# Crossbar transposes of z, split score exponentials and earlier PV steps in a fused attention and MLP kernel

## The chip, the core and the metric

The kernel runs on one core of a Trainium2 chip. The metric is the device time in microseconds (us) of one execution. Before the change it was 321.34 us, the median of three runs (319.71 to 322.16). Names used below: PE is TensorE, ACT is ScalarE, DVE is VectorE, POOL is GpSimd; SP is the engine whose queue issues most of the DMA transfers. The clock given with a profile is the share of TensorE's full clock that was granted; "half clock" means that this share was 0.5.

## The reference

```python
# q, k, v: (8 batches, 8 heads, 576 tokens, 64), fp32
scores = q @ k.T / 8, kept where 0 <= pos_q - pos_k < 64, else -1e9   # window of 64
attn   = softmax(scores) @ v                                          # per head
x      = attn, heads side by side: (8, 576, 512)
xn     = (x - mean) / sqrt(var + 1e-6) * g_ln
out    = x + relu(xn @ w_ch1) @ w_ch2                                 # 512 -> 2048 -> 512
```

## The kernel before

The kernel works in batches of 512 tokens. While TensorE runs the MLP of batch g, the attention of batch b = g + 1 runs beside it, in gaps that the program text fixes. (The last 64 tokens of all batches, the "tails", form a ninth MLP batch.) An MLP batch in the steady part is a row of 30 units: 16 first-layer units ("hps": four matmuls of 512 columns and one Relu on ScalarE), then 14 product units of eight 256-column matmuls (wX, wY, wZ). After each unit the program may place attention work in a slot. In the names of the tiles, sc are scores and pt their exponentials; PV is the product of pt with v, its result is xps; vA is v in fp16 and vB its copy shifted by 64 rows; xn is the attention's output, mv its mean and variance and rs the factor made from the variance; z is the normalized row block and zT its transpose, which the MLP reads. The "presums" are VectorE's sums and differences (sw1 to sw4) of parts of the first layer's result hrT, which the products need; osb is the output tile. The two hps buffers are what ties PE to ScalarE: a unit can start only when the Relu of the unit two before has emptied its buffer.

```python
def l1(hc):                                   # one hps unit
    hps = ps_mm.tile([128, 512], FP32, ...)   # pool of 2 buffers
    for kc in KCS: nc.tensor.matmul(out=hps, lhsT=w1g[...], rhs=zT[g][:, kc, :], ...)    # L409
    nc.scalar.activation(out=hrT[:, hc, :], in_=hps, func=AF.Relu, ...)                  # L413
# ... (cut)
def b_step(g, kb):                            # PV of one score step, then the norm's statistics
    # 16 matmuls xps <- pt, vA or vB (L313); VectorE: rcp, xn, stats, mv
def r_step(g, kb):                            # two tiny ScalarE instructions, wait for mv
    nc.scalar.activation(out=rs, in_=mvs[(g, kb)][:, 1:2], func=AF.Ln, ...)              # L332
    nc.scalar.activation(out=rs, in_=rs, func=AF.Exp, ...)                               # L333
def z_step(g, kb): ...                        # VectorE: z <- xn, mv, rs   (128 x 512, fp16)
def zt_step(g, kb):                           # 4 PE transposes and one ScalarE copy
    for kc in range(NKC): nc.tensor.transpose(out=ztp[:, kc, :], in_=z[...], ...)        # L357
    nc.scalar.copy(out=zT[g][:, :, 128 * kb:128 * kb + 128], in_=ztp)                    # L360
def make_vB(b):                               # shift of v by 64 rows, from GpSimd's queue
    nc.gpsimd.dma_start(out=vB[b][64:128, :], in_=vA[b][0:64, :])
    nc.gpsimd.dma_start(out=vB[b][0:64, 1:4], in_=vA[b][64:128, 0:3])
# ... the schedule of one steady batch (cut): slot numbers are units
for j in range(4):
    at((0, 6, 11, 17)[j], s_mm, b, j)         # scores and both exponentials
    at((1, 7, 12, 18)[j], s_mask, b, j)
    bz((6, 11, 17, 23)[j], b, j)              # b_step, then r_step and z_step one and two units on
    at((12, 17, 23, 28)[j], zt_step, b, j)
at(1, load_qk, n, 0); at(2, load_qk, n, 1); at(5, load_v, n, 0, 4)   # SP's queue, n = b + 1
at(11, x_main, n, 0); at(13, x_main, n, 1)                            # SP: crossbar transposes of q, k
at(26, make_vB, n)
```

In the traces here SP issues its transfers in the order of the program (below, the loads of 178.87 go out behind the transposes that stand before them), so a transfer that waits for its data holds up whatever the program has put behind it.

The softmax here doesn't subtract the row's maximum and nothing guards it: scores larger than these inputs give would overflow.

## Time and profile before

| | before |
|---|---|
| time, median of 3 runs | 321.34 us |
| span of the profiled run, clock | 319.0 us, 0.998 |
| steady batch, from its first hps matmul to the next one's | 30.95 us, four times |
| of it PE's short waits for a Relu | 0.645 us |
| of it the bare queue of PE | 30.31 us |

The third row is read from the start times of the first hps matmul of each batch. The fourth takes more care, because the modelled matmul ends hide short waits: for each unit I take the distance from its start to the next one's and subtract what the same kind of unit needs when nothing holds it. "Waits" below always means this excess. PE's own list of waits in this profile shows none of those 0.645 us.

### The profile page before, as it was taken

The numbers are of one execution on the slowest core, as the hardware profiler recorded it, in microseconds if no ns is written. First come the engines' busy times: TensorE is split into PE (matmuls) and PEld (weight loads), VectorE is DVE, ScalarE is ACT, GpSimd is POOL, SyncE is SP. The second block draws the span as 40 slices with busy tenths as digits, with TensorE's granted clock in tenths as the row PEclk, the third lists the DMA queues.
The fourth block names the chain that finished last, engine by engine and source line by source line (L and its number), as shares of the span: only waits on it lengthen the run. The fifth ranks groups of instructions, "written<-read, shape, count | busy, mean of one in ns | idle before, by whom it ended". The sixth has DMA issues, their size and how long they took to land.

```text
span 319.0 us, 7507 instructions
## 1 busy us (share of the span) xinstructions
PE 296.9 (93%) x3047; PEld 195.5 (61%) x3047; DVE 207.4 (65%) x365; ACT 170.9 (54%) x345; POOL 128.6 (40%) x212
## 2 busy tenths in 40 slices
PE   6879998789989999999999999999999999899993
PEld 2446444378766458646864685578457854684582
DVE  0564569965996569457935893689288956771361
ACT  1699734268534763477257715851685277415600
POOL 3676667653535433452246225613444061201000
PEclk9999999999999999999999999999999999999999
DMA  7999999999997979795979688940988979203005
GB/s 177 257 369 303 333 286 288 286 285 216 142 211 159 262 117 243 145 268 135 197 153 236 149 184 211 194 101 1 251 161 143 181 188 164 51 0 134 0 2 132
DMA packets 127379, 58.35 MB, mean 183 GB/s; under 512 B 104496, under 2 KB 120368, under 8 KB 127344
## 3 DMA queue, kind: packets, MB, share of 16 engines
q1 hardware_dynamic: 123280, 46.15, 66.2%
q0 software_dynamic: 3104, 11.19, 11.4%
q10 hardware_dynamic: 960, 0.53, 0.6%
q8 instruction: 24, 0.39, 0.6%
q14 instruction: 11, 0.09, 0.1%
HBM read 38.80 MB, written 9.44 MB: 151 GB/s over the span
## 4 chain that ended last, share of the span: by engine, by line
PE 49%; DVE 12%; DMA 9%; SPq 5%; ACT 4%; issue 3%; POOL 1%; POOLq 0%
PE hps L409 19%; PE wX L483 12%; DMA tk<-in_k_dram 6%; PE wZ L483 6%; PE hph L443 3%; PE wY L483 3%; SPq L102 2%; PE xps L313 2%; DMA tv<-in_v_dram 2%; PE sc L280 2%; DVE sw L399 2%; DVE osb L498 2%; DVE stats L321 2%; DVE xn L319 2%; DVE pt L297 1%
## 5 line engine op out<-in xcount | busy, mean ns | idle before, releaser
L409 PE MATMUL hps<-zT,w1g 128*128 128x512 f16 x480 | 112.3, 379 | 1.4 <-ACT zT L360 0.3
L413 ACT ACTIVATE hrT<-hps 128x512 f16<-128x512 f32 x120 | 71.3, 596 | 31.0 <-PE hps L409 30.1
L409 PEld LDWEIGHTS <-w1g 128*128 128x128 f16 x480 | 45.0, 98 | 54.1 <-issue 6.9
L483 PEld LDWEIGHTS <-sw 128*128 128x128 f16 x512 | 49.3, 98 | 7.5 <-issue 1.1
L483 PEld LDWEIGHTS <-hrT 128*128 128x128 f16 x384 | 36.6, 98 | 6.2 <-issue 0.3
L360 ACT COPY zT<-ztp 128x512 f16<-128x512 f16 x36 | 21.0, 584 | 33.1 <-PE ztp L357 32.9
L399 DVE TENSOR_TENSOR sw<-hrT 128x1024 f16<-128x1024 f16 x32 | 22.3, 696 | 24.7 <-ACT hrT L413 24.6
L332 ACT ACTIVATE rs<-mv,epst 128x1 f32<-128x1 f32 x36 | 10.7, 296 | 44.6 <-DVE mv L323 44.6
L297 DVE TENSOR_TENSOR pt<-pt,mask 128x1024 f16<-128x1024 f16 x32 | 24.6, 772 | 14.2 <-ACT pt L284 9.2
L131 POOL CAST qk<-qk 128x1024 f16<-128x1024 f32 x22 | 23.8, 1083 | 11.9 <-DMA qk<-in_q_dram 8.6
L349 POOL CAST tok<-hrT 128x1 f32<-128x1 f16 x29 | 11.9, 410 | 37.4 <-ACT hrT L413 27.5
L443 PE MATMUL hph<-zT,w1g 128*128 128x256 f16 x192 | 23.9, 273 | 2.6 <-DVE osb L432 1.7
L321 DVE BATCH_NORM_STATS2 stats<-xn 128x6 f32<-128x512 f32 x36 | 25.0, 695 | 1.2
L319 DVE TENSOR_TENSOR xn<-xps,rcp 128x512 f32<-128x512 f32 x36 | 24.9, 692 | 1.2
L498 DVE TENSOR_TENSOR osb<-wX,xn 128x512 f32<-128x512 f32 x24 | 16.5, 688 | 13.6 <-PE wX L483 13.6
L316 DVE RECIPROCAL rcp<-xps 128x8 f32<-128x8 f32 x36 | 7.3, 203 | 25.3 <-PE xps L313 25.3
L284 ACT ACTIVATE pt<-sc 128x512 f16<-128x512 f32 x40 | 21.7, 595 | 1.7
L150 POOL CAST vA<-v 128x512 f16<-128x512 f32 x32 | 22.1, 699 | 0.8 <-DMA v<-in_v_dram 0.8
L443 PEld LDWEIGHTS <-w1g 128*128 128x128 f16 x192 | 17.9, 98 | 6.0 <-issue 2.3
L370 POOL DMA_DIRECT2D out_dram<-osb x18 | 12.6, 700 | 20.5 <-DVE osb L498 17.1
L290 ACT ACTIVATE pt<-sc 128x512 f16<-128x512 f32 x32 | 17.2, 595 | 6.0 <-PE sc L280 5.7
L343 DVE TENSOR_SCALAR z<-xn,mv,rs 128x512 f16<-128x512 f32 x32 | 19.7, 615 | 0.9 <-ACT rs L333 0.6
(76 smaller groups left out, 432.2 us busy)
## 6 DMA issues: line engine op xcount, KB each, us to landing
qk<-in_q_dram SPq DMA_DIRECT2D x16, 512.0 KB, 6.2
v<-in_v_dram SPq DMA_DIRECT2D x32, 256.0 KB, 6.2
out_dram<-osb POOLq DMA_DIRECT2D x14, 512.0 KB, 7.1
w2s<-in_moe_w_ch_dram SPq DMA_DIRECT2D x12, 512.0 KB, 6.2
qk<-in_k_dram SPq DMA_DIRECT2D x20, 256.0 KB, 5.7
qk<-in_k_dram SPq DMA_DIRECT2D x6, 512.0 KB, 6.9
w1s<-in_moe_w_ch_dram SPq DMA_DIRECT2D x4, 512.0 KB, 6.6
tk<-in_k_dram SPq DMA_DIRECT2D x8, 256.0 KB, 5.3
```

Of the source, the lines that this page charges most:

```text
L131: nc.gpsimd.tensor_copy(out=dst[:, :].rearrange("p (a j) e d -> p a e j d", j=j), in_=t[:, :].rearrange("p (a e j d) -> p a e j d", e=2, j ...
L150: nc.gpsimd.tensor_copy(out=vA[b][:, c0:c1, :, 0:D], in_=v32[b][:, c0:c1])
L284: nc.scalar.activation(out=pt[:, par].rearrange("k h w (p j) -> k (h w) p j", j=4), in_=sc[par][:, :].rearrange("k h w (j p) -> k (h w) p ...
L297: nc.vector.tensor_tensor(out=ptv, in0=ptv, in1=mb, op=ALU.mult)
L319: nc.vector.tensor_tensor(out=xn, in0=xps[:, :, 0:D], in1=rcp_b, op=ALU.mult)
L321: nc.vector.bn_stats(out=stats, in_=xn.rearrange("p h d -> p (h d)"))
L399: nc.vector.tensor_tensor(out=S[i], in0=a, in1=b, op=op)
L409: nc.tensor.matmul(out=hps, lhsT=w1g[:, kc, 128 * hc:128 * (hc + 1)], rhs=zT[g][:, kc, :], start=(kc == KCS[0]), stop=(kc == KCS[-1]),)
L413: nc.scalar.activation(out=hrT[:, hc, :], in_=hps, func=AF.Relu, bias=0.0, scale=1.0)
L443: nc.tensor.matmul(out=hps[:, e], lhsT=w1g[:, kc, 128 * hc:128 * (hc + 1)], rhs=zT[g][:, kc, 256 * half:256 * half + 256], start=(kc == KC ...
L483: nc.tensor.matmul(out=xyz[bank][:, t], lhsT=lhsT, rhs=rhs, start=bool(first and t == 0 and hc == 0), stop=(t == 1 and hc == 7), skip_grou ...
L498: nc.vector.tensor_tensor(out=o, in0=xyz[bank][:, ts], in1=x if base == "x" else o, op=ALU.add)
```

## The change

Its intent: take the sixteen groups of z transposes of the attention of batches 3 to 6 (which runs beside MLP batches 2 to 5) off PE and give them to the DMA crossbar; let a Relu in between the two exponentials of a score step; and move the PV steps forward, so that the transposed z is early enough.

```diff
-    def s_mm(g, j, pe_mask=False, pool=None):
+    def s_mm(g, j, pe_mask=False, pool=None, split=False):
 ...
+            if par == 0 or not split:
+                s_exp(g, j, par, sc[par])          # the second one comes a unit later
 ...
+    def x_step(g, kb):
+        nc.sync.dma_start_transpose(out=zT[g][:, :, 128 * kb:128 * kb + 128], in_=z)
 ...  presums of the products, slots
-                    (6, 3, 0), (10, 3, 1), (13, 1, 0), (14, 2, 0), ..., (20, 4, 0), (22, 4, 1)):
+                    (4, 3, 0), (10, 3, 1), (12, 1, 0), (12, 2, 0), ..., (22, 4, 0), (23, 4, 1)):
-                at((0, 6, 11, 17)[j], s_mm, b, j)
-                at((1, 7, 12, 18)[j], s_mask, b, j)
-                bz((6, 11, 17, 23)[j], b, j)
-                at((12, 17, 23, 28)[j], zt_step, b, j)
+                cross = g < B - 2
+                u, ub = ((0, 4, 8, 13)[j], (4, 8, 13, 18)[j]) if cross else ((0, 6, 11, 17)[j], (6, 11, 17, 23)[j])
+                if u < 15:
+                    at(u, s_mm, b, j, False, None, True)
+                    at(u + 1, s_exp, b, j)
+                    at(u + 2, s_mask, b, j)
+                else:
+                    at(u, s_mm, b, j)
+                    at(u + 1, s_mask, b, j)
+                bz(ub, b, j)
+                if cross:
+                    at(ub + 3, x_step, b, j)
+                else:
+                    at((12, 17, 23, 28)[j], zt_step, b, j)
 ...  and the tokens that pace GpSimd's casts of v: rs and the output tile in place of zT
```

More of the change, by code (lines that the diff above doesn't have):

```diff
@@ L282, in s_mm, with s_exp @@
         for par in range(2):
-            if NPE <= g < NGRP - 1:
-                nc.scalar.activation(
-                    out=pt[:, par].rearrange("k h w (p j) -> k (h w) p j", j=4),
-                    in_=sc[par][:, :].rearrange("k h w (j p) -> k (h w) p j", j=4),
-                    func=AF.Exp, bias=0.0, scale=scale,
-                )
-            else:
-                nc.scalar.activation(out=pt[:, par], in_=sc[par], func=AF.Exp, bias=0.0, scale=scale)
+            if par == 0 or not split:
+                s_exp(g, j, par, sc[par])
+        if split:
+            scs[(g, j)] = sc[1]
+    scs = {}
+    def s_exp(g, j, par=1, sc=None):
+        sc = scs.pop((g, j)) if sc is None else sc
+        pt = pts[(g, j)]
+        if NPE <= g < NGRP - 1:
+            nc.scalar.activation(
+                out=pt[:, par].rearrange("k h w (p j) -> k (h w) p j", j=4),
+                in_=sc[:, :].rearrange("k h w (j p) -> k (h w) p j", j=4),
+                func=AF.Exp, bias=0.0, scale=scale,
+            )
+        else:
+            nc.scalar.activation(out=pt[:, par], in_=sc, func=AF.Exp, bias=0.0, scale=scale)
     def s_mask(g, j):
@@ L362, in zt_step @@
             nc.vector.tensor_copy(out=dst, in_=ztp)
+    def x_step(g, kb):
+        z = zsd.pop((g, kb))
+        if g not in zT:
+            zT[g] = p_grp.tile([128, NKC, 512], FP16, tag="zT", name=f"zT_{g}")
+        nc.sync.dma_start_transpose(out=zT[g][:, :, 128 * kb:128 * kb + 128], in_=z)
     stores, cur = [], [0]
@@ L387, in t_weights @@
         nc.vector.tensor_tensor(out=o, in0=a, in1=b, op=ALU.subtract)
-    hrTs, sw = {}, {}
+    hrTs, sw, oo_of = {}, {}, {}
     def presum(g, i, c):
@@ L415, in mlp_units @@
         ch, oo = {}, {}
+        oo_of[g] = oo
         def l2(kb, part):
@@ L720 @@
             for u, i, c in ((10, 3, 0), (12, 3, 1), (14, 1, 0), (15, 2, 0), (16, 1, 1), (17, 2, 1), (20, 4, 0), (22, 4, 1)) if g == 1 else (
-                    (6, 3, 0), (10, 3, 1), (13, 1, 0), (14, 2, 0), (16, 1, 1), (17, 2, 1), (20, 4, 0), (22, 4, 1)):
+                    (4, 3, 0), (10, 3, 1), (12, 1, 0), (12, 2, 0), (16, 1, 1), (17, 2, 1), (22, 4, 0), (23, 4, 1)):
                 at(u, presum, g, i, c)
@@ L724 @@
             for j in range(4):
-                at((0, 6, 11, 17)[j], s_mm, b, j)
-                at((1, 7, 12, 18)[j], s_mask, b, j)
-                bz((6, 11, 17, 23)[j], b, j)
-                at((12, 17, 23, 28)[j], zt_step, b, j)
+                cross = g < B - 2
[10 more added lines that the diff above has]
+                    at(ub + 3, x_step, b, j)
+                else:
+                    at((12, 17, 23, 28)[j], zt_step, b, j)
         for i, f, *p in TAILS.get(g, ()):
@@ L770 @@
                 at(18, alloc_vB, n)
-                for u, c, j in ((18, 0, 1), (20, 1, 2), (24, 2, 2), (26, 3, 3)):
-                    at(u, (lambda j=j: pace(zT[b][:, 0, 128 * j:128 * j + 1])) if c % 2 == 0 else
-                       (lambda j=j: pace(rss[(b, j)])))
+                for u, c, t in ((18, 0, lambda: rss[(b, 2)]), (20, 1, lambda: oo_of[g][0][:, 0, 0:1]),
+                                (22, 2, lambda: rss[(b, 3)]), (25, 3, lambda: oo_of[g][1][:, 0, 256:257])):
+                    at(u, lambda t=t: pace(t()))
                     at(u, cast_v, n, c, c + 1)
```

## The prediction

> **What bounds the kernel now.** I read the page first (busy time by engine), then busy time by stretches of one batch each, then the chain of work that ended last, then the timelines of TensorE (PE) and ScalarE (ACT) inside one batch.
>
> ```profile
> PE 296.9 (93%) x3047; PEld 195.5 (61%) x3047; DVE 207.4 (65%) x365; ACT 170.9 (54%) x345; POOL 128.6 (40%) x212
> 131.50:162.40 30.90, 30.73 (x322) 20.30 (x320) 20.93 (x39) 17.32 (x36) 12.22 (x24) 1.00 0.81 186
> 193.40:224.30 30.90, 30.73 (x322) 20.30 (x320) 20.95 (x39) 17.32 (x36) 12.51 (x24) 1.00 0.60 130
> ```
>
> The last two lines are batches 3 and 5 of the MLP (columns: length, busy PE, PEld, DVE, ACT, POOL, then clock, DMA share, GB/s). PE has no visible idle time, so the batch length is what PE's own queue adds up to; the starts of the first hps matmuls are 30.95 us apart in batches 2 to 5. The DMA share differs (0.81, 0.60) at equal length: DMA doesn't set it. But matmul ends are modelled, so short waits hide in "busy". Start-to-start distances show them:
>
> ```profile
> 175.31 1.08 ACT L284 ACTIVATE pt<-sc 128x512 f16<-128x512 f32 x2
> 176.29 0.60 ACT L413 ACTIVATE hrT<-hps 128x512 f16<-128x512 f32 x1
> 176.78 0.59 ACT L360 COPY zT<-ztp 128x512 f16<-128x512 f16 x1
> 177.25 0.31 ACT L332 ACTIVATE rs<-mv,epst 128x1 f32<-128x1 f32 x1
> 177.59 0.20 ACT L333 ACTIVATE rs<-rs 128x1 f32<-128x1 f32 x1
> 177.70 1.14 ACT L413 ACTIVATE hrT<-hps 128x512 f16<-128x512 f32 x2
> ```
> ```profile
> 176.09 0.39 PE L357 MATMUL ztp<-ident,z 128*128 128x128 f16 x4
> 176.31 3.04 PE L409 MATMUL hps<-zT,w1g 128*128 128x512 f16 x12
> 179.19 1.04 PE L483 MATMUL wX<-w2s,hrT 128*128 128x256 f16 x8
> ```
>
> The hps matmuls follow each other every 0.216 us, 0.863 for a unit of four. The twelve at 176.31 should need 2.59 and the next group starts 2.88 later: 0.29 of waiting. Above it is why: hps has two buffers, so a unit can start only after the Relu of the unit two before; the Relu (ready 0.2 after its unit's end, 0.6 long, PE resumes 0.05 after its end) has about 0.01 of slack. Two exponentials, a zT copy and the two little rs instructions stood before it. The other two waits of a batch, read the same way, are 0.205 (after the first score step's exponentials, Relu 165.00 to 165.62, PE at 165.67) and 0.15 (exponentials, then rs, at 171.00 to 172.05). Together 0.645 us per batch.
>
> **What the Trainium skill says.** "Perfetto Trace Analysis", § Identifying the Most-Contended Engine, calls matmul busy share a poor measure because matmuls are pipelined. Agreed here: one hps matmul is shown as 379 ns, yet they start every 216. "TensorE: Matmul & The Clock Gate", § Architectural detail, says ScalarE and VectorE queues are strict FIFO. The trace agrees: rs at 171.62 begins 0.04 after mv's end (171.58), and the Relu behind it, ready at 171.87, begins at 172.05. "VectorE: DVE Perf Modes", § The three transpose paths, gives 1309 ns for a 128x128 transpose by the DMA crossbar against 390 ns on TensorE. Here four TensorE transposes occupy PE for 0.223 (176.09 to 176.31). "DMA: Bandwidth & Descriptors", § Rules for kernel authors, says that a transpose next to ordinary DMAs needs no extra wait; all of these are issued from one queue, and the trace has them already for q and k:
>
> ```profile
> qkT<-qk SPq DMA_TRANSPOSE x30, 2.9
> ```
>
> **The change part by part.** It touches batches 3 to 6 of the attention, which run beside MLP batches 2 to 5, and in part batch 7 (beside MLP 6).
>
> 1. Removed: 16 groups of four PE transposes and 16 ACT copies. PE: 16 x 0.223 = 3.57 us, all on the path, 0.89 per batch. ACT's 16 x 0.59 frees mostly product phases where ACT is idle.
>
> 2. Added: 16 crossbar transposes of 128x512 on SP's queue. The existing ones of that size issue in 1.25 and land 2.5 to 4.4 after they start. SP per batch: six transposes at about 1.3 to 2, loads of q and k 6.5, of v 5.5, plus 4 x 1.3 = about 26 of 31 us. As SP works in order, the q/k transposes now wait for the second z and the next q/k loads for the fourth. I followed it: fourth PV after unit 18, at about 21 us into the batch; z by 25; landed by 28; first read at 31. Loads then start at 26 instead of 16.4, land by 37, and are cast from 35 on in that order. Enough, with 2 to 3 us to spare. Load: 4 x 128 KB in packets of 256 B are 2048 more per batch, beside 12400 now. Hidden, 0.
>
> 3. Splitting the exponentials. First score step (unit 0; zero = start of the first hps matmul): Relu 1 is no longer behind both. Second exponential starts 2.87, frees ACT at 3.34; Relu 2 is ready at 3.24, ends 3.94, unit 4 starts 3.99 instead of 3.90. Waiting 0.095 instead of 0.205.
>
> 4. Moving PV to units 4, 8, 13. This is where the gain goes. In the built kernel ACT's order around unit 5 is: Relu 5, rs Ln, rs Exp, second score exponential, Relu 6, and likewise at units 9 and 14. The rs pair of unit 5 waits for mv, which ends 2.37 after PV's start (169.215 to 171.58), and the exponential stands behind it. With PV at 4.95 (unit 4's end 4.86 + 0.09), sc 5.33, unit 5 at 5.67, unit 6 at 6.54, unit 7 at 7.41: Relu 5 from 6.74; mv 7.32; Ln 7.35; Exp 7.68; score exponential 7.79; ACT free 8.27. Relu 6, ready at 7.61, runs 8.27 to 8.87, unit 8 starts at 8.92 instead of 8.27: 0.65 lost. The same sum at unit 9 (PV 9.88, mv 12.25, exponential 12.72, Relu 10 13.20 to 13.80, unit 12 at 13.85 instead of 13.19): 0.66. At unit 14 it delays only Relu 15; unit 16 writes another buffer (X), so nothing is lost.
>
> 5. The moved presums: VectorE's order after unit 16, laid out with 0.6 per step, delivers sw2 at 21.6 (needed 22.1) and sw4 at 27.0 (needed 27.3). No wait, but only 0.3 to 0.5 to spare.
>
> Sum per batch 2 to 5: waits 0.095 + 0.65 + 0.66 = 1.41 instead of 0.645, so +0.76; transposes -0.89; net -0.13, four times -0.5. MLP batch 6 keeps its PE transposes but gets the split with rs at units 7 and 12 ahead of the exponential: -0.11, then +0.5 twice, +0.9. Of this up to 0.75 is absorbed by the wait for the last tail's transposed keys that PE has anyway (1.72 instead of 0.98 for eight wX matmuls and their switch at 273.1), since tail loads may start 1 us earlier. Last batches: +0.1. Total -0.5 + 0.4 + 0.1 = about 0 us.
>
> **The rivals.** (a) *The gain comes through*: the split removes the waits as intended and PE loses 16 x 0.223 + 4 x 0.645 = 6.2 us, giving 315. For it: PE is the bound and ACT is only 54% busy. Against it: the order of ACT's queue, and the wait of rs on mv that the chain already shows between exponentials and Relu. Half of that, 318, if the waits come out near 0.3. (b) *DMA becomes the bound*: the share rises from 0.81 to 0.9 and z, q/k and loads form one queue; a late zT, or a late vB shift (now landing 4.6 to 5.2 after issue, PV at unit 4 about 1.6 after that) would cost 1 to 2 us per batch: 325 to 329. For it: vB's slack falls by two units and q/k loads now overlap it. Against: equal batch lengths at shares of 0.6 and 0.9, 311 GB/s reached in a stretch against a mean of 186. (c) *VectorE is late* with sw2 or sw4: 0.3 per batch, 322 to 323.
>
> **Range and chances.** Centre: 321.3 - 0.1 = 321.2. The wait sums could be off by 0.3 per batch either way (1.2 to 1.5 in all), runs of before spread over 319.7 to 322.2, and rivals (a, half) and (b, mild) pull by about 3 in each direction: 318.3 to 324.5 for 8 in 10. Faster by over 2% needs 314.9, only rival (a) in full: 0.05. Slower by over 2% needs 327.8, rival (b) in every batch: 0.04. Within 2%: 0.91.
>
> **What would show each step.** ztp groups fall from 36 to 20 and hps starts lie 30.8 apart (31 to 31.4 for rival c; 29.4 for a; over 32 for b). In ACT's timeline a Relu following Ln, Exp, exponential, with unit 8 starting about 0.65 late and unit 12 too, and unit 4 only 0.1 late. zT transposes landing before the next batch's first hps with 2 us left; PE's waits naming zT, qkT or vB would refute step 2. If ACT ran the score exponential before the rs pair, step 4 would be wrong and the time near 317.

## More of the kernel before

What the prediction doesn't show is SP's queue in one batch, which will matter (start, time to issue, line, transfer; lines of the timeline of SP):

```profile
169.11 3.10 SPq L233 DMA_TRANSPOSE qkT<-qk  x1
...
176.27 2.54 SPq L239 DMA_TRANSPOSE qkT<-qk  x2
178.87 0.57 SPq L83 DMA_DIRECT2D qk<-in_q_dram  x1
...
183.84 1.57 SPq L90 DMA_DIRECT2D qk<-in_k_dram  x2
```

The six crossbar transposes of q and k follow each other from 169.11, and the next batch's q and k loads are all issued by 185.41, 23 us into a batch that began at 162.43. After that the queue is nearly empty until the batch ends at 193.38.

## The result, and the profile after

| | before | after |
|---|---|---|
| median, runs of the same round (4 each) | 321.68 us | 324.89 us |
| range | 319.71 to 322.16 | 324.12 to 325.5 |
| profiled span | 319.0 us | 323.5 us |
| steady batches | 30.95 four times | 31.09, 31.22, 31.16, 32.14 |

The ratio is 1.011 (95% interval 1.0061 to 1.0159): 1.1% slower. Ratios here are the mean time of one kernel's fast runs over that of the other's of the same rounds, so not quite the ratio of the medians. The state of a one-core run is judged by its time alone (slow: over 1.5% above the fastest of the same kernel).

Busy PE of the page, then of two batches, the second and fourth with crossbar transposes (length; busy PE, PEld, DVE, ACT, POOL; clock, DMA share, GB/s):

```profile
PE 294.9 (91%) x2983; PEld 191.5 (59%) x2983; DVE 217.0 (67%) x365; ACT 162.0 (50%) x329; POOL 127.6 (39%) x212
132.59:163.81 31.22, 30.07 (x307) 19.28 (x304) 22.63 (x39) 15.11 (x32) 12.28 (x24) 1.00 0.85 186
194.96:227.10 32.14, 30.07 (x306) 19.30 (x304) 22.63 (x39) 15.11 (x32) 12.54 (x24) 1.00 0.97 196
```

PE has less to do in a batch (30.07 busy against the 30.73 that the prediction shows) and yet the batch is longer. PE has begun to wait. The list of PE's waits now shows it (what it waited for: us in total, times, longest):

```profile
PE hps L425 <- ACT hrT L429: 5.1, 10, 0.6
...
PE xps L323 <- DMA vB<-vA: 1.1, 1, 1.1
...
PE sc L280 <- DMA tkT<-tk: 0.8, 1, 0.8
PE hps L425 <- ACT zT L370: 0.8, 1, 0.8
```

The first line is the Relu waits, no longer hidden. Here is one of them on ScalarE, unit 5 and on:

```profile
170.68 0.60 ACT L429 ACTIVATE hrT<-hps 128x512 f16<-128x512 f32 x1 [0.38 <-PE hps L425]
171.29 0.30 ACT L342 ACTIVATE rs<-mv,epst 128x1 f32<-128x1 f32 x1
171.62 0.20 ACT L343 ACTIVATE rs<-rs 128x1 f32<-128x1 f32 x1
171.73 0.58 ACT L294 ACTIVATE pt<-sc 128x512 f16<-128x512 f32 x1
172.20 1.07 ACT L429 ACTIVATE hrT<-hps 128x512 f16<-128x512 f32 x2
```

and on PE:

```profile
169.61 2.76 PE L425 MATMUL hps<-zT,w1g 128*128 128x512 f16 x12
172.84 1.02 PE L425 MATMUL hps<-zT,w1g 128*128 128x512 f16 x4 [0.47 <-ACT hrT L429]
```

The order is Relu 5, rs pair, second exponential, Relu 6, as predicted. Three units need 3 x 0.863 = 2.59 us; the fourth starts 172.84 - 169.61 = 3.23 later, so 0.64 is lost at unit 8 (predicted 0.65). At unit 12 it is 0.70 (predicted 0.66), at unit 4 0.10 (predicted 0.095).

What was not predicted is in the other lines and in SP's queue:

```profile
177.63 2.97 SPq L378 DMA_TRANSPOSE zT<-z  x2
180.69 2.29 SPq L233 DMA_TRANSPOSE qkT<-qk  x1
...
187.05 2.54 SPq L239 DMA_TRANSPOSE qkT<-qk  x2
189.69 2.53 SPq L378 DMA_TRANSPOSE zT<-z  x2
192.27 0.57 SPq L83 DMA_DIRECT2D qk<-in_q_dram  x1
...
194.06 3.96 SPq L83 DMA_DIRECT2D qk<-in_q_dram  x1
198.06 4.36 SPq L90 DMA_DIRECT2D qk<-in_k_dram  x2
202.52 6.56 SPq L144 DMA_DIRECT2D v<-in_v_dram  x4
209.19 2.97 SPq L378 DMA_TRANSPOSE zT<-z  x2
```

The next q and k loads start at 192.27, 28.5 us into a batch that began at 163.81; their issue lasts until 202.42, well into the next one. GpSimd issues the shift of v at 193.53, right beside them. From 126.7 us to the end of the last of these batches (227.1) SP's queue has no pause above 0.3 us: it goes round once in 31.6 us (177.63 to 209.19). In the kernel before it pauses twice in each of these batches, for 2 to 3 and for 5 to 12 us. The DMA issues, before and then after (KB each, median us to landing):

```profile
vB<-vA POOLq DMA_DIRECT2D x6, 260.0 KB, 5.0
vB<-vA POOLq DMA_DIRECT2D x6, 195.0 KB, 6.4
```
```profile
vB<-vA POOLq DMA_DIRECT2D x6, 260.0 KB, 6.4
vB<-vA POOLq DMA_DIRECT2D x6, 195.0 KB, 7.5
...
zT<-z SPq DMA_TRANSPOSE x16, 2.5
```

The z transposes themselves land in 2.5 us, but the shift of v takes 1.1 to 1.4 us longer than before, and PV, which moved two units forward, waits for it: 0, 0.20, 0.13 and 1.12 us in the four batches. The slack of the last z transpose before the next batch shrinks from batch to batch: it lands 3.4, 2.1, 1.5 and 0.8 us ahead of the next hps.

**Where the difference of 4.45 us between the two spans is.** First two batches, whose code is the same: +0.96 (this run has two stretches of 3.4 us at half the TensorE clock there, at 8.6 and 90.6 us; the run of before has none, so I count this as noise). The four crossbar batches: +1.81. MLP batch 6 (which gets only the split): +1.37. Batch 7: +0.31. Without the noise that is 3.49, and the medians are 324.89 - 321.68 = 3.21 us apart.

### The profile page after: what moved, and what is told of

Read it like the earlier page. It is cut to its first block, busy times and chain, and to the rows that moved or that the text cites.

```text
span 323.5 us, 7390 instructions
## 1 busy us (share of the span) xinstructions
PE 294.9 (91%) x2983; PEld 191.5 (59%) x2983; DVE 217.0 (67%) x365; ACT 162.0 (50%) x329; POOL 127.6 (39%) x212
## 2 busy tenths in 40 slices
DMA packets 136082, 60.43 MB, mean 187 GB/s; under 512 B 113200, under 2 KB 129072, under 8 KB 136048
## 3 DMA queue, kind: packets, MB, share of 16 engines
q0 software_dynamic: 3104, 11.19, 11.1%
## 5 line engine op out<-in xcount | busy, mean ns | idle before, releaser
L429 ACT ACTIVATE hrT<-hps 128x512 f16<-128x512 f32 x120 | 70.4, 596 | 60.1 <-PE hps L425 59.9
L500 PEld LDWEIGHTS <-sw 128*128 128x128 f16 x512 | 50.3, 99 | 8.5 <-issue 1.2
L307 DVE TENSOR_TENSOR pt<-pt,mask 128x1024 f16<-128x1024 f16 x32 | 26.7, 837 | 17.3 <-ACT pt L294 13.0
L415 DVE TENSOR_TENSOR sw<-hrT 128x1024 f16<-128x1024 f16 x32 | 25.6, 800 | 17.6 <-ACT hrT L429 17.6
L359 POOL CAST tok<-hrT 128x1 f32<-128x1 f16 x29 | 10.6, 365 | 47.6 <-ACT hrT L429 38.6
L353 DVE TENSOR_SCALAR z<-xn,mv,rs 128x512 f16<-128x512 f32 x32 | 21.4, 667 | 6.8 <-ACT rs L343 6.2
L294 ACT ACTIVATE pt<-sc 128x512 f16<-128x512 f32 x40 | 23.5, 589 | 3.2 <-PE sc L280 1.8
L323 PEld LDWEIGHTS <-pt 128*64 128x64 f16 x576 | 12.2, 110 | 16.3 <-DVE pt L307 5.5
L150 POOL CAST vA<-v 128x512 f16<-128x512 f32 x32 | 21.1, 668 | 1.2 <-DMA v<-in_v_dram 1.2
L300 ACT ACTIVATE pt<-sc 128x512 f16<-128x512 f32 x32 | 17.3, 594 | 6.3 <-PE sc L280 6.0
L323 PE MATMUL xps<-vB,pt 128*64 128x65 f16 x256 | 14.4, 198 | 5.0 <-DVE pt L307 3.1
```

What stands on the lines that cost most here:

```text
L294: nc.scalar.activation(out=pt[:, par].rearrange("k h w (p j) -> k (h w) p j", j=4), in_=sc[:, :].rearrange("k h w (j p) -> k (h w) p j", j=4),
L307: nc.vector.tensor_tensor(out=ptv, in0=ptv, in1=mb, op=ALU.mult)
L323: nc.tensor.matmul(out=xps[64 * r:64 * r + 64, h, :D + 1], lhsT=pt[:, par, hp, r, :], rhs=rhs, start=True, stop=True)
L353: nc.vector.tensor_scalar(out=z, in0=x, scalar1=mv[:, 0:1], scalar2=rss[(g, kb)][:, 0:1], op0=ALU.subtract, op1=ALU.mult)
L415: nc.vector.tensor_tensor(out=S[i], in0=a, in1=b, op=op)
L500: nc.tensor.matmul(out=xyz[bank][:, t], lhsT=lhsT, rhs=rhs, start=bool(first and t == 0 and hc == 0), stop=(t == 1 and hc == 7), skip_grou ...
```

## The experiments

My theory after the result: the ScalarE waits are as predicted, and the DMA step was not free. The first rival: the split alone costs everything and the crossbar is fine. The second: the v shift alone is at fault, through its place in the schedule. Later rivals are named where they arise. All eighteen kernels gave correct results. Batch lengths are those of MLP batches 2 to 5 in the profiled run.

### Which part costs what (one chip, 3 rounds)

**rs_late**: the rs pair and z one unit later, so that no rs stands before the second exponential.

```diff
-                bz(ub, b, j)
+                at(ub, b_step, b, j)
+                late = 1 if ub < 15 else 0
+                at(ub + 1 + late, r_step, b, j)
+                at(ub + 2 + late, z_step, b, j)
-                    at(ub + 3, x_step, b, j)
+                    at(ub + 3 + late, x_step, b, j)
```

> The changed kernel with the rs pair (and z and the zT transpose behind it) of the PV steps before unit 15 one unit later, so that the second score exponential stands directly behind its Relu and the rs pair behind the next one. Theory 1 (most of the loss is the queue Relu, Ln, Exp, exponential, Relu on ScalarE): the waits of 0.64 and 0.70 us per batch fall to about 0.1 each, so 1.1 us less in each of batches 2 to 5 and about 1.1 in batch 6: 319 to 320.5 us beside 324.9. Theory 2 (DMA: the late vB shift and the tail loads set the time): nothing gained but what is then waited for elsewhere, 323.5 or more. Theory 3 (VectorE late with post sums): about 324, and the wait before the third wX product stays at 0.18 or grows.

Measured: 327.15 us (324.6 to 328.75), ratio 1.02 (1.0143 to 1.0256). ScalarE now has the order in which exponential and Relu go first:

```profile
168.32 0.59 ACT L294 ACTIVATE pt<-sc 128x512 f16<-128x512 f32 x1
168.80 0.60 ACT L429 ACTIVATE hrT<-hps 128x512 f16<-128x512 f32 x1
169.28 0.30 ACT L342 ACTIVATE rs<-mv,epst 128x1 f32<-128x1 f32 x1
169.62 0.20 ACT L343 ACTIVATE rs<-rs 128x1 f32<-128x1 f32 x1
```

The waits at units 8 and 12 fell from 0.64 and 0.70 to 0.10 and 0.10, so this cause is shown. Three batches became 30.35, 30.56 and 30.72; they grow because PV's wait for v grows, 0.23, 0.50 and 0.66 (then 1.28). But the fourth became 38.22, with this line in PE's waits:

```profile
PE hps L425 <- DMA zT<-z: 6.7, 1, 6.7
```

Its fourth z transpose was issued at 221.55, 0.50 us after GpSimd's shift of v, and landed 7.77 us later instead of 2.5. PE idled, its clock was halved for 10.2 us from 224.9 on, and the first three units of the next batch took 0.8 to 1.1 longer each.

**no_split**: both exponentials together again, everything else as changed.

```diff
-                if u < 15:
-                    at(u, s_mm, b, j, False, None, True)
-                    at(u + 1, s_exp, b, j)
-                    at(u + 2, s_mask, b, j)
-                else:
-                    at(u, s_mm, b, j)
-                    at(u + 1, s_mask, b, j)
+                at(u, s_mm, b, j)
+                at(u + 1, s_mask, b, j)
```

> The changed kernel with both exponentials of a score step together again, all else as changed. Theory 1: the queue in front of a Relu is again rs pair alone or two exponentials alone; waits per batch 0.205 + 0.15 + 0.15 = 0.5 instead of 1.43, so 0.9 us less in each of batches 2 to 5 and 0.8 in batch 6: 320 to 321 us. Theory 2 (DMA): 324 to 325 unchanged. If the split is what saves time and something else loses it: slower than 325.5.

Measured: 327.58 us: the fast runs are 322.86 and 325.51, the slow ones 329.66 and 330.08; ratio of the fast ones 1.0115 (1.005 to 1.0179). Batches 29.98, 31.25, 30.34, 37.27 (profile of a slow run). The first of them has nothing but 0.56 of Relu waits: this is the crossbar's full gain, 0.97 us below before; a fast run of a later kernel, nosplit_quiet, has the same length. The last has the same accident as rs_late, which showed it in a fast run. The view of the tile zT, over that end of the batch:

```profile
L378 SPq DMA_TRANSPOSE zT<-z x4: 1218/1457/2380, 208.8 to 222.6; - x4
...
DMA to landing us min/median/max: 2.6/3.7/7.9
```

The longest is again the fourth, issued 0.43 us after the shift of v. So the first rival falls: without the split the crossbar loses its gain by itself. Two cautions. A run with this accident can count as slow (in the profiled one half-clock stretches of 10.2 and 3.4 us, together some 6.8 us of lost clock, account for most of what the clock of 0.975 lacks), so the ratio of the fast runs leaves part of it out. And the fast run of 322.86 had a clock of 0.994, too high for a stretch of 10 us at half clock (an estimate: that alone would give 0.984), so it can hardly have had the whole accident. Still it was not below the kernel before; no profile of it is kept, and what held it is open.

**shift_early**: v cast in one burst at units 18 to 21, its shift at unit 22 instead of 26.

```diff
+                at(18, lambda: pace(rss[(b, 2)]))
+                for u, c in ((18, 0), (19, 1), (20, 2), (21, 3)):
                     at(u, cast_v, n, c, c + 1)
-                at(26, make_vB, n)
+                at(22, make_vB, n)
```

> The changed kernel with the four casts of v at units 18 to 21 in one go and the vB shift issued at unit 22 instead of 26, about 3 us before the next q and k loads are issued. Theory 2 (the vB shift is late because it now shares the DMA engines with the q and k loads): the shift lands 4.5 to 5.5 us after issue again instead of 6.4 to 7.4, well before PV; the waits of PV at unit 4 (0.2, 0.13 and 1.12 us in batches 3 to 5) are gone: about 1.4 us less, 323 to 323.8. Theory 1 alone: these waits are small in other executions, and the time stays within 0.3 us of 324.9.

Measured: 324.34 us, ratio 1.0129 (1.009 to 1.0168). PV's waits for v are gone (0.14 in one batch, else 0), yet batches are 31.75 to 32.01, because the products now wait for VectorE: 0.44 to 0.55 at unit 20 and 0.46 at unit 23. Whether the burst of casts on GpSimd slowed VectorE, or only its order did, no run tells. The second rival falls in this form: moving the shift swaps one wait for another.

**split_only**: the kernel before, with nothing but the split.

```diff
+                cross = False
```
(with presums and pacing tokens as before)

> The kernel before with the exponentials of the score steps before unit 15 one unit apart, nothing else. Theory 1: with PV at units 6 and 11 the rs pair again stands before the second exponential; waits per batch 0.1 + 0.64 + 0.77 = 1.5 instead of 0.645, so 0.87 us more in each of five batches (2 to 6): about 325.5 to 326 us. If the split relieves ScalarE's queue as intended: 0.1 to 0.6 us less per batch, 318.5 to 321.

Measured: 325.41 us, ratio 1.0145 (1.0103 to 1.0188), batches 31.82 four times.

```profile
PE hps L425 <- ACT hrT L429: 4.3, 8, 0.6
```

The waits of a batch are 0.10, 0.64 and 0.77, 1.50 instead of 0.64: the split costs 0.87 us a batch, without any crossbar transpose.

### Loads from another queue, and the transposes back on PE (same chip, 3 rounds)

**pe_transposes**: the changed kernel with the z transposes on PE.

```diff
-                    at(ub + 3, x_step, b, j)
+                    at(ub + 6, zt_step, b, j)
```

> The changed kernel with the rows of batches 3 to 6 transposed on TensorE again (PV at 4, 8, 13, 18, exponentials apart). If the crossbar transposes save their 0.89 us per batch on TensorE and cost little elsewhere: ScalarE's waits stay (0.1, 0.64, 0.7, a little more with the zT copies) and the batches take about 31.9 us, 326 to 327.5 in all, slower than the changed kernel by 1 to 2.5. If the crossbar part loses as much by late vB and zT as it saves: 324 to 325.5.

Measured: 325.29 us, ratio 1.017 (1.0108 to 1.0233), batches 31.63 four times. Against after (mean 31.40) the crossbar is worth 0.22 a batch of the 0.89 that it takes off PE.

**nosplit_pez**: pe_transposes with both exponentials together, so of the change only the moved PV steps, presums and pacing are left.

> The changed kernel with TensorE's transposes and with both exponentials together again: only the PV units, the presum units and the pace of the v casts are as changed. By the sums: waits about 0.2 + 0.15 + 0.2 to 0.4, batches of 30.8 to 31.2 us, like the kernel before: 320 to 322 us. If moving PV by itself costs: 323 or more.

Measured: 318.83 us (318.44 to 320.79; before in these rounds 320.63), ratio 0.9975 (0.9916 to 1.0034), batches 30.75 four times: the moved PV steps, with their presums and pacing, gain 0.20 a batch.

**loads_pool** and **rslate_pool**: is SP too long a queue? The q and k loads of the next batch go out from GpSimd's queue at unit 12, in the changed kernel and in rs_late.

```diff
-            at(e, load_qk, n, 0)
-            at(e + 1, load_qk, n, 1)
+            if g < 3:
+                at(e, load_qk, n, 0)
+                at(e + 1, load_qk, n, 1)
+            if g > 1 and n + 1 < B:
+                at(12, load_qk, n + 1, 0, nc.gpsimd)
+                at(12, load_qk, n + 1, 1, nc.gpsimd)
```

> The changed kernel with the q and k loads from batch 5 on issued from GpSimd's queue at unit 12, nothing else. Theory A: PV's waits for the vB shift (0.2, 0.13, 1.12 us in batches 3 to 5 of the profile) go, at least those of batches 4 and 5; ScalarE's waits of 0.64 and 0.70 stay: 323 to 324 us. Theory B: no change, 324.5 to 325.5.

> rs_late (the rs pair one unit later) with, from batch 5 of the attention on, the q and k loads of the next batch issued from GpSimd's queue at unit 12, right after the casts that free their buffers, instead of from SP's queue behind the fourth z transpose. Theory A (in rs_late PE was freed, but SP's queue, in order and slowed by loads that collide with the vB shift and the stores, delivered zT and vB late, and the idle TensorE then lost half its clock for 10 us): SP's queue has 6 of 20 transfers less, zT lands 3 us or more before the next batch, the shift lands in about 5 us, no wait of 6.9 us, no half clock; batches of 30.0 to 30.4 us: 315 to 317.5 us. Theory B (the DMA engines themselves are full, whoever issues): zT and vB stay late, 322 us or more.

Measured: 376.03 us (ratio 1.1729) and 368.55 us (1.1259). It is the opposite of a cure. PE's waits in loads_pool from 95 to 240 us:

```profile
PE hps L425 <- DMA zT<-z: 38.2, 2, 20.4
```

The third and fourth z transposes, in SP's queue, landed 10 to 14 us after their issue in the two worst batches of loads_pool, and 17.2 and 21.3 us in the worst of rslate_pool; the q and k transposes ahead of them in SP's queue were late as well (up to 24 us).

### The order in SP's queue (another chip, 3 rounds)

**sp_order**, **nosplit_sporder**, **rslate_sporder**: the loads stay on SP but go before the third z transpose (units 12 and 13), the q and k transposes move to units 6 and 10; alone, with no_split, with rs_late.

```diff
-            at(e, load_qk, n, 0)
-            at(e + 1, load_qk, n, 1)
+            if g < 3:
+                at(e, load_qk, n, 0)
+                at(e + 1, load_qk, n, 1)
+            if g > 1 and n + 1 < B:
+                at(12, load_qk, n + 1, 0)
+                at(13, load_qk, n + 1, 1)
-                at(11, x_main, n, 0)
-                at(13, x_main, n, 1)
+                at(6, x_main, n, 0)
+                at(10, x_main, n, 1)
```

> The changed kernel with another order on SP's queue only: q and k transposes at units 6 and 10 (behind their casts, no longer behind the second z transpose), the next batch's q and k loads (from batch 5 on) at units 12 and 13, ahead of the third z transpose. Theory A (the z transposes made SP's order late, the loads then meet the vB shift and the stores, and PV waits for the shift): PV's waits of 0.2, 0.13 and 1.12 us fall to about 0, zT lands over 2 us early; ScalarE's 0.1 + 0.64 + 0.70 stay; batches about 31.0 us: 323 to 324 us. If order on SP doesn't matter: 324.5 to 325.5.

> The same order on SP together with both exponentials of a step together. Theory A plus theory 1 (the split costs 0.87 us per batch on ScalarE's queue, SP's order costs the rest): waits 0.2 + 0.15 + 0.2, batches of 30.0 us in all of batches 2 to 5, no wait of 7 us before batch 6, no half clock: 316 to 318 us, faster than the kernel before by 0.8 to 1.4%. If the crossbar part can't pay because the DMA engines are full: 320 or more, with zT or vB waits.

> The same order on SP, exponentials apart as changed, rs pair one unit later. Theory A plus theory 1: waits 0.1 + 0.1 + 0.1 + 0.3 (third wX product), batches of 30.0 to 30.1 us, batch 6 at about 33, no half clock: 316 to 318 us. This is the changed kernel with only the two faults of order mended; 322 or more would refute that order is the fault.

Measured: 331.93 (ratio 1.0364), 339.0 (1.0491) and 337.19 us (1.0416). A miss. PV's waits for v are gone in all three, but the third and fourth z transposes now stand behind the loads in the same queue: PE waits at the end of a batch, 1.87, 2.81 and 1.34 us in sp_order, 5.5 to 7.7 in nosplit_sporder, 1.6 to 8.0 in rslate_sporder: where the rest of the batch is shorter, this wait is longer. A wait of 2.81 was followed by a half-clock stretch, one of 1.87 was not.

**nosplit_quiet**: no_split with GpSimd's shift and stores held back by three units, in the one batch that had the accident.

```diff
-                stores.append((cur[0], nc.gpsimd, dst, oo[p]))
+                stores.append((cur[0] + (3 if g == 5 else 0), nc.gpsimd, dst, oo[p]))
-                at(26, make_vB, n)
+                at(29 if g == 5 else 26, make_vB, n)
```

> no_split with GpSimd's transfers at the end of MLP batch 5 (vB shift and the two stores) held back by three units, so that they don't run beside the fourth z transpose of that batch; nothing else. Theory C (a crossbar transpose in 256 byte packets starves beside GpSimd's 4 KB packets: 7.9 us instead of 2.5): that transpose lands in 2.5 to 4.5 us, the wait of 6.96 us and the half clock behind it go, all executions at 318.5 to 322 us instead of 323 to 330. If something else made it late: as no_split.

Measured: 326.33 us (322.43 to 327.12), ratio 1.0164. Half a confirmation: the transpose of that batch now lands in 4.14 us instead of 7.92 and its wait is gone. But the accident turned up one batch earlier (5.75 us, then 6.8 us of half clock), and that wait also set the slip back: the transpose that landed in 4.14 us was issued 27.0 us into its batch, in no_split 29.3. So the run doesn't part the two.

### What stayed open after twelve runs: collision, order, or no room at all (a third chip, 3 rounds)

**nosplit_quietall**: as nosplit_quiet, in all four batches.

> The changed kernel with the two exponentials of a score step together, the shift of the v tile at unit 29 and the stores of GpSimd three units later, in all four crossbar batches. If the long waits for the zT tile come from transfers of the GpSimd queue that lie beside the fourth z transpose (collision): no wait at unit 29 above 1.5 us in any of batches 3 to 6, the fourth transpose lands in under 5 us each time, PV waits for the v tile instead (0.5 to 3 us per batch); 318 to 323 us. If the transposes are late because the SP queue has more to do in a batch than the batch is long (order): waits of 3 to 7 us at unit 29 appear in at least one batch all the same; 324 us or more.

Measured: 325.05 us, two of four runs slow; fast ones 321.02 and 323.75, ratio 1.0087 (0.9995 to 1.0178). Batches 29.98, 29.97, 36.91, 32.06. The profile is of a slow run, and there a wait of 6.51 us at unit 29 comes all the same, as the expectation gave to order: the transposes had slipped so far that the fourth, issued at 190.90, met the shift of v at 191.21 although that was held back, and landed 8.11 us later. The third, issued at 189.59, landed in 2.50. The clock was full until 197.2. But of the fast runs 321.02 lies where the expectation has collision and 323.75 between the two theories: holding GpSimd back may help, and not in every run.

**nosplit_actx**: no_split with the q and k loads from ScalarE's queue at unit 17, and the q and k transposes (which the expectations call "x loads") at units 6 and 10 instead of 11 and 13; of the edit, the loads:

```diff
+            if g > 1 and n + 1 < B:
+                at(17, load_qk, n + 1, 0, nc.scalar)
+                at(17, load_qk, n + 1, 1, nc.scalar)
```

> The changed kernel with the exponentials together, the q and k loads of the next batch issued from the ScalarE queue at unit 17 and the x loads at units 6 and 10. If the order of the SP queue is the cause: z transposes issue at once behind the z tile, no wait at unit 29, batches of 30.0 to 30.3 us, 315.5 to 318 us. If the transposes starve beside any loads of large packets (capacity or arbitration, whoever issues them): the fourth transpose takes 6 us or more beside the q and k loads, waits of 2 us or more at unit 29, 324 us or more.

Measured: 322.1 us (one of four runs slow), ratio 1.0067 (1.0005 to 1.0129), batches 32.12, 33.73, 32.04, 29.92 (the profile is of the slow run). PE doesn't wait for zT at all, as order says. But neither theory had thought of ScalarE: issuing six loads held it from 121.13 to 128.14, so rs came late, then VectorE (which waited 2.3 us for rs), then PE (up to 2.0 us for VectorE's output add), all in the first of these batches. The last three z transposes beside those loads took 4.55 to 7.25 us there. The last batch has no such loads, and is the shortest steady batch of all profiles.

**nosplit_two** and **nosplit_twox**: the crossbar only for the first two score steps of a batch, PE for the last two, exponentials together; in the second one also the q and k transposes at units 6 and 10.

```diff
-                    at(ub + 3, x_step, b, j)
+                    at(ub + (3 if j < 2 else 6), x_step if j < 2 else zt_step, b, j)
```

> The crossbar only for the first two score steps of a batch, TensorE for the last two, exponentials together. Both theories have no transpose near the end of a batch to be late: waits at unit 29 gone, half of the removed 0.89 us kept, batches of 30.2 to 30.5 us, 316.5 to 318.8 us. If instead the loss is in the transposes' effect on the shift of the v tile and the loads (every crossbar transpose slows the other transfers), PV still waits 0.5 us or more per batch and batches stay at 30.7 us or above; 319 us or more.

> As the kernel with two crossbar steps, with the x loads at units 6 and 10 in place of 11 and 13. Order: the loads of x no longer stand behind the second transpose, PV waits for the v tile are gone or under 0.1 us, 0 to 1 us shorter than its twin, 316 to 318.5 us. Collision or capacity: x loads beside the first two transposes make those land late; no gain over the twin or up to 1.5 us longer.

Measured: nosplit_two 322.13 us (one of four runs slow), ratio 1.0072 (0.9995 to 1.015), batches 30.42, 31.83, 31.38, 30.59, with PV waiting 0, 1.42, 0.96 and 0.19 for v. nosplit_twox 318.89 us, ratio 0.9991 (0.9934 to 1.0048), batches 30.42 three times and 31.03. With no z transpose near the end of a batch the accident is in neither profile. The waits for v go in three of four batches when the q and k transposes stand earlier in the queue; 0.63 is left in the fourth, and MLP batch 6 ends with a wait 0.95 longer than in nosplit_pez (1.66 against 0.71).

### Is the crossbar worth anything then (a fourth chip, 5 rounds)

**two_late5**: nosplit_twox with the q and k transposes of the last one (beside MLP batch 5) back at units 11 and 13, against those two waits. **pez_beside**: the code of nosplit_pez, as its control on the same chip.

```diff
-                at(6, x_main, n, 0)
-                at(10, x_main, n, 1)
+                at(6 if g < 5 else 11, x_main, n, 0)
+                at(10 if g < 5 else 13, x_main, n, 1)
```

> The kernel with two crossbar steps a batch and early x loads, with batch 6's loads of x back at units 11 and 13, so that the end of the run is as in the twin with late x loads. If what is left of the loss is where the loads stand in the queue: four batches of 30.4 to 30.6 us, batch 7's stretch 32.5 to 32.7 us instead of 33.5, no wait of PV for the v tile above 0.3 us in batches 3 to 5; 316.5 to 318.3 us, ratio to the kernel before 0.988 to 0.996, and 0.5 to 1.5 us below its control without any crossbar step. If every crossbar transpose costs about what it saves wherever it stands: no difference to the control (within 0.5 us).

> The control on the same chip: the same code as the TensorE kernel with the exponentials together (no crossbar step at all). Both theories: four batches of 30.75 us, 318 to 319 us, ratio to the kernel before 0.993 to 0.999. It sets what the two crossbar steps of the other kernel are worth.

Measured: two_late5 318.73 us (317.05 to 321.94, one of six runs slow), ratio to before 0.9965 (0.9914 to 1.0016). pez_beside 320.44 us (319.14 to 322.17), ratio 1.0028 (0.9979 to 1.0077). Against each other the means of the fast runs are 318.67 and 320.49, so two_late5 is 1.82 us below its control, barely clear of the scatter of the runs (95% interval about 0.1 to 3.6); its ratio is just above the 0.988 to 0.996 that was expected, and so is the control's above its 0.993 to 0.999. Two of its batches:

```profile
130.80:161.21 30.41, 30.33 (x314) 19.72 (x312) 22.86 (x39) 16.18 (x34) 12.81 (x24) 1.00 0.95 197
191.63:222.04 30.41, 30.33 (x314) 19.71 (x312) 22.86 (x39) 16.18 (x34) 13.07 (x24) 1.00 0.65 143
```

All batches are equal, at DMA shares of 0.95 and 0.65, and the q and k loads are issued by 187.25, 26.0 us into the batch begun at 161.22 (before: 23). SP's queue then pauses for 2.67 us, and earlier in that batch for 2.92. It is the best version that I found, 0.35% below the kernel before with an interval that includes no gain; against the changed kernel, measured on another chip, it is about 1.4% faster by the two ratios (0.9965 / 1.011 = 0.986).

### The batches side by side

| kernel | batch | waits | batch less waits |
|---|---|---|---|
| before | 30.95 | 0.64 | 30.31 |
| nosplit_pez: PV moved, no split, PE transposes | 30.75 | 0.44 | 30.31 |
| split_only | 31.82 | 1.50 | 30.32 |
| pe_transposes: PV moved, split | 31.63 | 1.32 | 30.31 |
| after (mean of four) | 31.40 | 1.99 | 29.41 |
| nosplit_quiet: no split, first two batches | 29.98 | 0.56 | 29.42 |
| two_late5: two crossbar steps | 30.41 | 0.55 | 29.86 |

The last column knows only three values: the bare queue of PE with sixteen, eight and no z transposes in a batch. Everything else is in the waits.

## Why the prediction was right or wrong

The range was 318.3 to 324.5; measured were 324.89 us. The class, within 2%, was right; the range was missed by 0.4.

**Step 1, removed PE transposes: right.** Predicted 0.89 a batch; the bare queue fell from 30.31 to 29.41, 0.90.

**Step 2, "Hidden, 0": this is the step that failed.** It followed the deadline of zT and asked whether each transfer is in time on its own duration of before. On that it was nearly right: in the changed kernel every zT landed before its use, by 3.4 down to 0.8 us where it said 2 to 3. But its sum of SP's queue, "about 26 of 31 us", kept the issue times of before: in the batch from 163.81 the issues take 31.1 us (q and k loads 10.1 instead of 6.3, v 7.1 instead of 5.3, q and k transposes 8.5, z 5.3). Why the same loads take longer to issue no run shows. The queue is full, and so everything in it comes later. And the prediction left out whom the shifted transfers meet. With the loads moved from 16.4 to 28.5 us into the batch they run beside GpSimd's shift of v, and the slack of "about 1.6" for that shift was eaten: 0.36 us a batch on average, 1.12 at worst (in one profiled execution). That is the sign by which the prediction wanted to see this step refuted, PE's waits naming vB. nosplit_pez has no such wait and two_late5 has none, so it comes from the crossbar steps and from what they push back in SP's queue. Rival (b) named this very shift and its shrunken slack, but argued it away with the DMA share. The share was the wrong measure: two_late5 has a batch at 0.95 with no wait, and after one at 0.85 with waits. So in these runs the total share doesn't tell which batch waits; order and neighbours do better.

**Step 3, first score step: right.** 0.10 measured for 0.095.

**Step 4, the rs pair before the exponential: right.** 0.64 and 0.70 measured for 0.65 and 0.66. rs_late removes the cause and the waits with it; split_only shows the same cost in the old schedule.

**Step 5, presums: right for the presums, too narrow for VectorE.** No product waited for sw2 or sw4. But at unit 23 a product waited for VectorE to finish an output add (osb): 0.25, 0.18, 0.18, 0.18, 0.20 us a batch on average. This is rival (c) in small, through another tile.

**The sum of a batch.** Waits were to be 1.41 and were 1.99: 0.10 + 0.64 + 0.70 = 1.43 (rounding aside), plus 0.36 for v and 0.20 for VectorE. With 0.90 saved, a batch is 0.45 longer on average instead of 0.13 shorter, so four cost 1.8 instead of gaining 0.5.

**Batch 6 and the end: the cost right, the absorption wrong.** The waits of the split in batch 6 were as predicted: 0.64 and 0.77, that is +0.49 and +0.48 where the prediction has +0.5 twice. But 0.50 more came at unit 29 (0.97 instead of 0.47, PE waiting for the ScalarE copy of zT behind a busy VectorE). And the prediction let the later wait for the tail's keys absorb up to 0.75, since "tail loads may start 1 us earlier". They did not: in the queue they stand behind the z transposes, their first loads began at 223.38 instead of 209.62 (28.4 us into batch 5 instead of 16.2), and that wait grew from 0.75 to 0.90. In split_only and pe_transposes, which have no crossbar steps, it is absent, and batch 7 takes 30.04 and 30.21 instead of 30.79: the absorption was right for the split and undone by step 2. Predicted +0.5 for all this, measured 1.37 + 0.31 = 1.68.

Together: 2.3 us too little in the four batches and 1.2 at the end make 3.5, which is the error: predicted 0.1 below before, measured 3.2 above (3.49 in the profiles, noise removed). Two slips of the prediction don't matter to this: its parts add up to about 0 while its centre takes off 0.1, and the 12400 packets "now" of a batch are 10,368 to 14,329 in the trace.

**What lies behind step 2, and how far it is shown.** Shown, in part: (1) with the crossbar the SP queue of a batch is as long as the batch (31.1 us of issues in one of 31.16). When other waits are taken out (no_split, rs_late), PE becomes faster than SP's cycle and the transposes slip: the fourth is issued 24.7, 27.2, 27.3 and 29.3 us into its batch in no_split, 24.5, 26.6, 27.2 and 30.4 in rs_late, against 25.2, 26.7, 27.2 and 27.2 in the changed kernel; in the third or fourth batch it is late. The waits in the changed kernel hid this, so curing the ScalarE waits alone could not bring the gain. (2) A crossbar transpose lands in 2.5 us alone and in 4 to 8 us, in the worst kernel about 20, when a transfer of another queue is issued close to it: GpSimd's in no_split, rs_late and nosplit_quietall, ScalarE's in nosplit_actx. A neighbour from another queue isn't needed for all of it: right behind loads of SP's own queue they took 4.0 to 5.3 us in the changed kernel with no other queue near (from 177.63, for one), and the third of a batch 5.0 to 7.6 in sp_order and nosplit_sporder, where the shift of v came in towards its end. By these traces the two act together: the slip brings a transpose to where its neighbour is. No run parts them cleanly, as in nosplit_quiet, where one went from 7.92 to 4.14, the neighbour and the slip were both gone. Holding GpSimd back in every batch saved the fast runs of nosplit_quietall in part only (321.02 and 323.75, before 319.93).

Only argued: why the transpose starves. The Trainium skill, "DMA: Bandwidth & Descriptors", § Queues, rings and completion order, says that a DMA engine takes turns between the queues that have work for it, one packet at a time. The 16 transposes added 136,082 - 127,379 = 8,703 packets and 2.08 MB, 239 bytes each; GpSimd's queue moves 11.19 MB in 3,104 packets, 3.6 KB each. If turns go by these packets, a transpose would get about one part in sixteen of the bytes while it has such a neighbour (an estimate). The durations fit this in direction, and the shift of v itself landed sooner in the two accidents than before (3.05 and 3.12 us, against a median of 5.0). But a packet of that page holds several descriptors, no run shows that the profile counts the same packets, and none changed their size.

Still open: whether all four crossbar steps of a batch could pay with a different order of all transfers. The order of the change and that of sp_order on SP, and loads from two other queues, did not do it.

## What to carry to other kernels

When work moves from a busy engine to a DMA queue, write out that whole queue over one cycle: if its cycle comes near the period of the kernel, the gain makes it late, and a lateness that grows from batch to batch shows only after several. Ask of each transfer not only whether it has time but which transfers of other queues will now run beside it; here half as many crossbar steps, placed in the quiet half of the batch, kept 0.34 us a batch of the 0.45 that they take off PE (30.41 against 30.75 in the control). And before splitting an instruction in two to let another in between, look at what already stands at the place to which the second half moves.

## What the Trainium skill lacked or had wrong

- "DMA: Bandwidth & Descriptors", § Rules for kernel authors, says that a transpose next to ordinary DMAs needs nothing. All outputs here were correct, so there the runs agree; but the page gives no slowdown for a transpose beside other queues, and here it is large: 2.5 us to landing for a 128x512 transpose alone, 7.3 to 8.1 us beside GpSimd's shift of v, 10 to 21 us in the worst batches with six loads in GpSimd's queue.
- The same page and section says that spreading transfers over issuing engines only saves issue time. Here moving six loads from SP's queue to GpSimd's made the kernel 16% slower than the changed one (ratios 1.1729 and 1.011; sp_order, with the loads at nearly the same units on SP and other transposes moved too, 1.0364), and moving them to ScalarE's cost that engine 7.0 us a batch (121.13 to 128.14).
- "VectorE: DVE Perf Modes", § The three transpose paths, compares the paths by the duration of one transpose (1309 ns by crossbar, 390 on TensorE). What decided here is not in that section: four transposes cost PE 0.22 us of its queue, and a crossbar transpose of 128x512 costs the 1.2 us or more that it occupies in the issuing queue, ahead of the loads behind it.
- "TensorE: Matmul & The Clock Gate", § Part 1: The HAM clock gate, says that the clock falls to half after an idle window of about 3.4 us. The runs mostly agree (waits of 5.5 to 7.7 us were followed by half-clock stretches of 6.8 and 10.2 us), but here less was enough: a wait of 2.81 us in sp_order and one of 2.15 in nosplit_actx were followed by half clock for 3.4 us, while one of 1.87 in sp_order, and two more of about 2.15 in nosplit_actx, were not. In the 3.4 us before these two stretches PE was busy for 1.29 and 1.43 us by the profile, so it hadn't been idle throughout.
